# A first sweep put in another order: the loads of two chunks ahead of a weight quarter, and state steps ahead of a scan and a transpose

## The chip, the cores and the metric

The kernel runs on one core of a Trainium2 chip. Its engines each work through a stream of their own, in order, and wait for each other only through semaphores: TensorE (PE in the profile, with its weight loads as PEld), VectorE (DVE), ScalarE (ACT), GpSimd (POOL) and SyncE (SP), which issues nearly all loads and stores. The metric is the device time of one execution in microseconds, and the median of several runs is compared.

## The reference

The input goes through a Mamba-2 style recurrence with decay, and then through a two-layer network with a tanh GELU. The recurrence works on 4 batches with 8 heads, a sequence of 768, heads of 32 and a state of 16:

```python
cum = np.cumsum(la, axis=-1)                                  # la: log of the decay a, inside a chunk
M = np.einsum('bhin,bhjn->bhij', Cc, Bc) * np.exp(cum_i - cum_j) * causal
y_intra = np.einsum('bhij,bhjd->bhid', M, xc)
y_inter = np.einsum('bhin,bhnd->bhid', Cc, state) * np.exp(cum)[..., None]
y[:, :, sl] = y_intra + y_inter
state = decay_full * state + sum_j(Bc * xc * decay_from_j)
...
x = y as (3072 tokens, 256)
h = x @ w_in                                                  # 256 x 2048
g = 0.5 * h * (1 + tanh(c * (h + 0.044715 * h**3)))
return g @ w_out                                              # 2048 x 256
```

## The kernel before

The sequence of each batch is cut into 6 chunks of 128, 24 chunks in all, and two chunks make a unit, 12 units u. Each unit of 256 tokens goes through the recurrence and then through the network. Everything is cut into named steps, and a step is one Python function that issues a few instructions on one engine (lines 777 to 960 name the steps and their engines). The string `ORDERED` (line 17) is the schedule: it lists the steps in the order in which their functions are called. Since an engine takes its instructions in that order, the string fixes the order on each engine, and on SP the order of the loads. A suffix (`:A`, `:D`, `:P`) puts a step on ACT, DVE or POOL in place of its usual engine, and `~n` issues filler matmuls. The framework adds the semaphores that the data need; a DMA that takes a semaphore used by an earlier one waits for that one to land.

The steps that the change and the prediction touch:

- **Loads.** `load_wi.q` (L190) brings a quarter of w_in, 512 KB, for the columns q*512 and on. `load_bc1.i` (L154) brings B (i = 0) or C (i = 1) of chunks 4 and 5 of batch 0, 128 KB each, in pieces of 128 bytes. `load_bc0` did so for chunks 0 to 3 at the start. `load_bc.b.i`, `load_x.u` and `load_wo.q` bring B or C of a later batch, a unit's x, and a quarter of w_out.
- **Casts.** `wi.q.k` and `wo.q.k` (L343, L346) turn half a quarter of the weights into bf16, mostly on POOL; `castx.u` does so for x.
- **Decay.** `clip` and `R` (L385, L388) make the decay products of all batches by a scan along each row. `tp2` (L391) transposes those of chunks 4 and 5 in four instructions, `tp6` (L399) those of the other batches, and `recip1`, `recip.b` invert them. `pe` (L406) picks the decay at the chunk ends, `pp` (L413) spreads it over the partitions by a matmul, and `pend` (L419) copies it out of PSUM. Chunks 0 to 3 have their own, earlier `Rq`, `tpq`, `pendq`.
- **B and C of chunks 4 and 5.** `mul1.i` (L457) scales them, `T1.i` (L463) transposes them on TensorE, `bh1` and `ce1.e` (L480, L473) copy B and the two masked forms of C out of PSUM, and `N1`, `bn1` (L483, L490) make B's other form.
- **Unit steps.** `G.u` (L614) multiplies B with C, `M.u.i` (L627) masks the product, half i at a time, `S.u.k` (L692) carries the state over chunk 2u + k, `SP.c` (L704) forms the state that chunk c hands on, `D.u` (L644) adds up the chunk's own state, and `Y.u` (L657) gives the unit's output from the earlier state (L673) and the chunk itself (L682). `yev.u` copies it as bf16 into `xm`. For units 0 and 1, `XX.u`, `XD.u` and `xn.c` (L578 to L605) unpack x and do the work of `D`.
- **Network.** `s1.u.i` (L723) multiplies a unit with 256 columns of w_in, in four matmuls, and needs the w_in quarter (2i + 1) // 4, so s1.u.6 and s1.u.7 need the last one, q = 3. `gelu.u.i` (L735) takes the result from PSUM. `s2.u.k.q` (L740) multiplies with a quarter of w_out, `oev` copies out and `store` writes.

The PSUM tile `hp` has two buffers, which `s1`, `D`, `pp` and one half of `XX` share in the order of the schedule. A group that takes one waits until the step that reads the group before last is done.

Of the kernel before, what the change touches and what calls it, by code (L numbers as in the profile page):

```python
# [18 lines left out]
load_a.0 load_a.1 c_warm load_a.2:A load_a.3:A load_x4 c_sel c_cz c_bmask clipq load_wi.0 Rq tpq  # L19
recip0 c_m16 mulc.0 ~51 tw.1 ew.1.1:A mulc.1 tw.2 mulb c_sub c_unp c_ends ~4 tw.0 peq ew.0.2 ew.0.1  # L20
load_wi.1 ew.0.0:A ew.1.2 c_par ~4 G.0 x4.1 ew.1.0 x4.0:D M.0.0 ~4 ppq GE.2 GE.3 pendq XX.0 ME.2
XD.0 xn.1 ME.3 xn.0:D load_wi.2 SP.0 ~17 Y.0 wi.0.1:A wi.0.0:A S.0.0 clip R S.0.1 yev.0.0.2 wi.1.1
XX.1 XD.1 wi.1.0 tp2 wi.2.1 xn.2 s1.0.0 G.1 S.1.0 s1.0.1 xn.3 gelu.0.0 gelu.0.1 s1.0.2 gelu.0.2
M.1.1 wi.2.0 M.1.0 s1.0.3 gelu.0.3 s1.0.4 s1.0.5 recip1 S.1.1 gelu.0.4 gelu.0.5 SP.1 load_wi.3
wi.3.1 wi.3.0 load_bc1.1 s1.0.6 load_bc1.0 mul1.0:P SP.2 pe mul1.1:P T1.0 bh1:D tp6 Y.1 gelu.0.6 pp
load_wo.0 pend:D yev.1.0.2 T1.1 N1 wo.0.0 s1.0.7 load_x.2 ce1.1:D castx.2.None ce1.0:D recip.1
s1.1.0 bn1 SP.3 gelu.0.7 wo.0.1 G.2 D.2 gelu.1.0 S.2.0 s1.1.1 gelu.1.1 s2.0.0.0.o s1.1.2 gelu.1.2
s1.1.3 load_bc.1.1 SP.4 load_bc.1.0 M.2.1 M.2.0 gelu.1.3 load_wo.1 s2.0.1.0.o mul.1.0 s1.1.4
mul.1.1:P recip.2 load_x.3 gelu.1.4 wo.1.0 s1.1.5 wo.1.1 Y.2 gelu.1.5 castx.3.None s1.1.6 yev.2.0.2
T.1.0 s1.1.7 gelu.1.6 load_wo.2 E.1.0 T.1.1 s1.2.0 N.1 gelu.1.7 gelu.2.0 E.1.1 bn.1:D s1.2.1 F.1  # L30
s2.0.0.1.o wo.2.0 wo.2.1:D s1.2.2 gelu.2.1 s2.0.1.1.o D.3 G.3 S.3.0 gelu.2.2 s1.2.3 gelu.2.3 S.3.1
M.3.0 M.3.1 load_wo.3 load_x.4 wo.3.0:A s2.0.0.2.o s2.0.1.2.o wo.3.1 SP.6 s1.2.4 s1.2.5 castx.4.None
s2.0.0.3.o s2.0.1.3.o gelu.2.4 gelu.2.5 oev.0:D s1.2.6 Y.3 oev.1 yev.3.0.2:D s2.1.0.0.o s2.1.0.1.o
s2.1.0.2.o gelu.2.6 s2.1.0.3.o s1.2.7 S.4.0 oev.2 recip.3 S.4.1 s1.3.0 s2.1.1.0.o M.4.1 s2.1.1.1.o
gelu.3.0 s2.1.1.2.o gelu.2.7 s2.1.1.3.o s1.3.1 s1.3.2 gelu.3.1 gelu.3.2 oev.3:D s2.2.0.0.o
s2.2.0.1.o s1.3.3 gelu.3.3 s2.2.0.2.o load_bc.2.1 load_bc.2.0 s2.2.0.3.o mul.2.1:P s1.3.4 M.4.0
load_x.5 s1.3.5 gelu.3.4 mul.2.0:P castx.5.None:D SP.7 oev.4:D SP.8 SP.9 s2.2.1.0.o s2.2.1.1.o
gelu.3.5 s2.2.1.2.o s1.3.6 s2.2.1.3.o gelu.3.6 Y.4 load_wr.2.1 s1.3.7 oev.5:D s2.3.0.0.o yev.4.0.2
load_x.6 load_wr.2.0 S.5.0 gelu.3.7 s1.4.0 s2.3.0.1.o M.5.0 load_tr.2.1 gelu.4.0 SP.10 M.5.1 s1.4.1
s2.3.0.2.o castx.6.None s1.4.2 load_bn.2 gelu.4.1 load_tr.2.0 s1.4.3 store.0 s2.3.0.3.o gelu.4.2  # L40
# [961 lines left out]
```

## Time and profile before

| | |
|---|---|
| median of 3 runs | 117.01 us (116.45 to 117.2) |
| profiled execution | 116.76 us |
| its span (first to last instruction) | 115.0 us |
| granted TensorE clock | 1.0 |
| TensorE busy | 108.1 us, 94% of the span |
| ScalarE, VectorE, GpSimd busy | 70.0, 68.0, 25.9 us |
| HBM read and written | 11.07 MB, 3.93 MB |

The profile is of one execution. Busy times are sums over the span; an engine can be busy for most of it and still not be what the end waits for. The timeline gives start, duration and, in brackets, how long the engine stood before an instruction and what ended that time; where several semaphores were waited for, it names the one that came last by its own records. A DMA issue is shown with the time that SP took to issue it, and apart from that the time until its last byte landed.

### The profile page before, as it was taken

The page shows a single profiled execution, that of the slowest core. Times are in us where ns is not written, and L with a number is a line of the kernel's source. Part 1 is how long each engine was busy: PE and PEld are TensorE (multiplying, and loading weights), DVE is VectorE, ACT ScalarE, POOL GpSimd, SP SyncE. Part 2 cuts the span into 40 slices and gives each one's busy share as a digit, 9 for nine tenths or more (in the row PEclk, how much of TensorE's full clock was granted, in tenths as well). Part 3 has the DMA queues.
Part 4 walks back from the last instruction along what each step waited for, and adds up shares of the span by engine and source line. Part 5 has one row for each costly group of instructions (what it writes and reads, how often), then busy time and mean ns, then how long its engine had stood idle before and what let it go on. Part 6 is the DMA issues. An engine that isn't in the chain of part 4 may idle for free.

```text
span 115.0 us, 3377 instructions
## 1 busy us (share of the span) xinstructions
PE 108.1 (94%) x1421; PEld 91.7 (80%) x1421; DVE 68.0 (59%) x136; ACT 70.0 (61%) x133; POOL 25.9 (23%) x54
## 2 busy tenths in 40 slices
PE   6979888999999999999999999999999999999990
PEld 2235566888879997989989899889898898999970
DVE  6889998989974755969448491186750851010100
ACT  3159687687654455747675876456495576758620
POOL 7636856806439020201120030000000000000000
PEclk9999999999999999999999999999999999999999
DMA  0999979979994779997556922350003020001113
GB/s 24 231 309 336 332 212 191 317 132 321 215 238 101 141 177 203 196 272 175 88 131 150 209 62 85 111 86 0 0 9 134 0 71 26 0 0 55 42 62 120
DMA packets 43103, 16.00 MB, mean 139 GB/s; under 512 B 36688, under 2 KB 41552, under 8 KB 43088
## 3 DMA queue, kind: packets, MB, share of 16 engines
q1 hardware_dynamic: 42896, 15.70, 55.3%
q8 instruction: 11, 0.18, 0.7%
q10 hardware_dynamic: 192, 0.09, 0.3%
q14 instruction: 4, 0.03, 0.1%
HBM read 11.07 MB, written 3.93 MB: 130 GB/s over the span
## 4 chain that ended last, share of the span: by engine, by line
PE 82%; DVE 5%; DMA 4%; SPq 3%; issue 2%; ACT 2%; DVEq 0%
PE hp L732 35%; PE o_ps L750 34%; DMA x_t<-in_x_dram 4%; PE yb L750 3%; PE yb L673 3%; PE ga L618 2%; PE yb L682 2%; DVE m L628 1%; DVE sp_new L706 1%; SPq L164 1%; ACT gT L736 1%; SPq L151 1%; SPq L160 1%; DVE rt L364 1%; DVE r_t L354 1%
## 5 line engine op out<-in xcount | busy, mean ns | idle before, releaser
L736 ACT ACTIVATE gT<-hp 128x512 bf16<-128x512 f32 x96 | 54.3, 596 | 28.9 <-PE hp L732 28.6
L732 PE MATMUL hp<-xm,w_in_sb 128*128 128x256 bf16 x384 | 53.4, 273 | 1.1 <-DVE s_new L699 0.5
L750 PE MATMUL o_ps<-w_out_sb,gT 128*128 128x256 bf16 x352 | 46.8, 273 | 0.0
L732 PEld LDWEIGHTS <-w_in_sb 128*128 128x128 bf16 x384 | 41.2, 114 | 4.0 <-issue 2.7
L750 PEld LDWEIGHTS <-gT 128*128 128x128 bf16 x384 | 37.4, 98 | 4.1 <-issue 0.4
L341 DVE COPY o_sb<-o_ps 128x256 f32<-128x256 f32 x12 | 5.1, 425 | 26.9 <-PE o_ps L750 26.9
L628 DVE TENSOR_TENSOR m<-ga,tri 128x1024 bf16<-128x1024 f32 x12 | 14.6, 1216 | 0.0
L628 DVE TENSOR_TENSOR m<-gb,tri 128x1024 bf16<-128x1024 f32 x11 | 13.4, 1216 | 0.0
L339 POOL CAST x<-x_t 128x512 bf16<-128x512 f32 x8 | 6.0, 756 | 28.1 <-DMA x_t<-in_x_dram 24.4
L706 DVE SCALAR_TENSOR_TENSOR sp_new<-s_new,pend,bmask 128x256 bf16<-128x256 f32 x17 | 8.0, 483 | 0.1
L699 DVE SCALAR_TENSOR_TENSOR s_new<-s_new,pend,hp 128x64 f32<-128x64 f32 x13 | 3.5, 272 | 7.4 <-PE hp L651 7.3
L720 PE MATMUL yb<-wz 128*128 128x512 bf16 (+2 forms) x21 | 6.6, 455 | 1.1 <-DVE warm L226 1.1
L337 ACT ACTIVATE o_sb<-o_ps 128x256 f32<-128x256 f32 x10 | 3.8, 383 | 5.1 <-PE o_ps L750 3.8
L682 PE MATMUL yb<-m,x 128*32 128x128 bf16 x192 | 6.1, 220 | 0.0
L337 ACT ACTIVATE xm<-yb 128x512 bf16<-128x512 f32 x8 | 4.8, 596 | 1.3 <-PE hp L651 0.7
L720 PEld LDWEIGHTS <-wz 128*128 128x128 bf16 x21 | 2.3, 116 | 4.1 <-issue 2.1
L673 PE MATMUL yb<-ce,sp_new 128*32 128x128 bf16 x160 | 5.3, 221 | 0.0
L339 POOL CAST w_out_sb<-wf 128x512 bf16<-128x512 f32 x6 | 4.1, 692 | 4.7 <-DMA wf<-in_moe_w_out_dram 4.7
L618 PE MATMUL ga<-ce,bh 32*128 32x256 bf16 x48 | 4.7, 273 | 0.3 <-DVE par L289 0.3
L618 PE MATMUL gb<-ce,bh 32*128 32x256 bf16 x48 | 4.7, 273 | 0.0
L750 PE MATMUL yb<-w_out_sb,gT 128*128 128x256 bf16 x32 | 4.5, 273 | 0.0
L682 PEld LDWEIGHTS <-x 128*32 128x32 bf16 x192 | 3.7, 96 | 0.9 <-issue 0.9
(114 smaller groups left out, 75.0 us busy)
## 6 DMA issues: line engine op xcount, KB each, us to landing
out_dram<-o_sb SPq DMA_DIRECT2D x24, 128.0 KB, 2.0
x_t<-in_x_dram SPq DMA_DIRECT2D x20, 128.0 KB, 3.9
wf<-in_moe_w_in_dram SPq DMA_DIRECT2D x4, 512.0 KB, 7.0
wf<-in_moe_w_out_dram SPq DMA_DIRECT2D x4, 512.0 KB, 7.1
bc_t<-in_C_dram SPq DMA_DIRECT2D x3, 384.0 KB, 4.7
bc_t<-in_B_dram SPq DMA_DIRECT2D x3, 384.0 KB, 5.7
scr<-bc SPq DMA_DIRECT2D x4, 192.0 KB, 2.3
x_t<-in_x_dram SPq DMA_DIRECT2D x1, 512.0 KB, 4.4
```

The source lines that it names most:

```text
L337: nc.scalar.activation(o, i, AF.Copy)
L339: nc.gpsimd.tensor_copy(out=o, in_=i)
L341: nc.vector.tensor_copy(out=o, in_=i)
L618: nc.tensor.matmul(out=gbank(g)[:, 256 * k:256 * k + 256], lhsT=bh_of(2 * u + k)[gs], rhs=ce_of(2 * u + k)[gs], start=True, stop=True, til ...
L628: nc.vector.tensor_tensor(out=m_of(u)[:, 2 * i:2 * i + 2].rearrange("p g k e t -> p (g k e) t"), in0=gx[i].rearrange("p g (k t) -> p (g k) ...
L673: nc.tensor.matmul(out=y4[32 * j:32 * j + 32, k, w], lhsT=sp[:, 32 * h:32 * h + 32], rhs=ce_of(gc)[:, h % 2], start=first(j), stop=False, ...
L682: nc.tensor.matmul(out=y4[32 * j:32 * j + 32, k, w], lhsT=X16[u][:, k, 32 * h:32 * h + 32], rhs=m[:, h // 2, h % 2, :], start=first(j), st ...
L706: nc.vector.scalar_tensor_tensor(out=sp_new.rearrange("p (g d) -> p g d", g=4), in0=(XN[0][:, H * D:H * D + 64] if gc == 0 else state[("s" ...
L720: nc.tensor.matmul(out=t[:, 0:m * 128], lhsT=wz, rhs=w3.to_broadcast([128, m, 128]), start=True, stop=True, skip_group_check=True)
L732: nc.tensor.matmul(out=hp[:, j * T:(j + 1) * T], lhsT=w_in_k[:, w, q, k], rhs=xm[:, w, u * T:(u + 1) * T], start=(w == 0), stop=(w == 1))
L736: nc.scalar.activation(gts[u][:, 2 * i:2 * i + 2], hps.pop((u, i)).rearrange("p (j t) -> p j t", j=2), AF.Gelu_apprx_tanh)
L750: nc.tensor.matmul(out=ops[gc], lhsT=gts[u][:, fi, k * Q:(k + 1) * Q], rhs=w_out_sb[:, fi, :], start=(fi == 0 and (u > 0 or k == 0)), stop ...
```

## The change

Only the string `ORDERED` changes, in the part of the first w_in sweep (unit 0) and the first half of the second. `load_bc1.0` and `load_bc1.1`, in this order now, come ahead of `load_wi.3`. `S.0.1` comes ahead of `R`, `S.1.0` ahead of `tp2`, `SP.1` and `SP.2` ahead of and between `M.1.0` and `M.1.1`, which change places. `mul1.0` comes ahead of the casts of the last w_in quarter on POOL and `mul1.1` behind them. `T1.0`, `Y.1` and `pp` come ahead of `s1.0.6`, and `G.2` and `D.2` stay behind `s1.1.0`. `bh1` and `pend` go from VectorE to ScalarE, `yev.1` from ScalarE to VectorE. From `gelu.1.7` on the list is the same as before (the diff breaks its lines elsewhere).

```diff
-XD.0 xn.1 ME.3 xn.0:D load_wi.2 SP.0 ~17 Y.0 wi.0.1:A wi.0.0:A S.0.0 clip R S.0.1 yev.0.0.2 wi.1.1
-XX.1 XD.1 wi.1.0 tp2 wi.2.1 xn.2 s1.0.0 G.1 S.1.0 s1.0.1 xn.3 gelu.0.0 gelu.0.1 s1.0.2 gelu.0.2
-M.1.1 wi.2.0 M.1.0 s1.0.3 gelu.0.3 s1.0.4 s1.0.5 recip1 S.1.1 gelu.0.4 gelu.0.5 SP.1 load_wi.3
-wi.3.1 wi.3.0 load_bc1.1 s1.0.6 load_bc1.0 mul1.0:P SP.2 pe mul1.1:P T1.0 bh1:D tp6 Y.1 gelu.0.6 pp
-load_wo.0 pend:D yev.1.0.2 T1.1 N1 wo.0.0 s1.0.7 load_x.2 ce1.1:D castx.2.None ce1.0:D recip.1
-s1.1.0 bn1 SP.3 gelu.0.7 wo.0.1 G.2 D.2 gelu.1.0 S.2.0 s1.1.1 gelu.1.1 s2.0.0.0.o s1.1.2 gelu.1.2
-s1.1.3 load_bc.1.1 SP.4 load_bc.1.0 M.2.1 M.2.0 gelu.1.3 load_wo.1 s2.0.1.0.o mul.1.0 s1.1.4
-mul.1.1:P recip.2 load_x.3 gelu.1.4 wo.1.0 s1.1.5 wo.1.1 Y.2 gelu.1.5 castx.3.None s1.1.6 yev.2.0.2
-T.1.0 s1.1.7 gelu.1.6 load_wo.2 E.1.0 T.1.1 s1.2.0 N.1 gelu.1.7 gelu.2.0 E.1.1 bn.1:D s1.2.1 F.1
+XD.0 xn.1 ME.3 xn.0:D load_wi.2 SP.0 ~17 Y.0 wi.0.1:A wi.0.0:A S.0.0 clip S.0.1 R yev.0.0.2 wi.1.1
+XX.1 XD.1 xn.2 S.1.0 tp2 s1.0.0 G.1 SP.1 load_bc1.0 s1.0.1 wi.1.0 M.1.0 gelu.0.0 xn.3 s1.0.2
+gelu.0.1 gelu.0.2 s1.0.3 SP.2 M.1.1 wi.2.1 wi.2.0 mul1.0:P recip1 gelu.0.3 S.1.1 load_bc1.1
+load_wi.3 wi.3.1 s1.0.4 T1.0 load_wo.0 load_x.2 load_bc.1.1 gelu.0.4 s1.0.5 Y.1 pe gelu.0.5 pp
+wi.3.0 s1.0.6 mul1.1:P T1.1 bh1 tp6 yev.1.0.2:D ce1.1:D N1 pend gelu.0.6 bn1 ce1.0:D load_bc.1.0
+s1.0.7 wo.0.0 s1.1.0 G.2 load_wo.1 gelu.0.7 castx.2.None gelu.1.0 recip.1 SP.3 wo.0.1 D.2 S.2.0
+s1.1.1 M.2.0 s1.1.2 gelu.1.1 s2.0.0.0.o s1.1.3 SP.4 gelu.1.2 M.2.1 s2.0.1.0.o gelu.1.3 s1.1.4 s1.1.5
+mul.1.0 gelu.1.4 mul.1.1:P recip.2 wo.1.0 wo.1.1 load_x.3 Y.2 s1.1.6 T.1.0 E.1.0 castx.3.None
+gelu.1.5 yev.2.0.2 gelu.1.6 s1.1.7 T.1.1 s1.2.0 N.1 load_wo.2 gelu.1.7 gelu.2.0 E.1.1 bn.1:D s1.2.1
+F.1 s2.0.0.1.o wo.2.0 wo.2.1:D s1.2.2 gelu.2.1 s2.0.1.1.o D.3 G.3 S.3.0 gelu.2.2 s1.2.3 gelu.2.3
...
```

More of the change, by code (lines that the diff above doesn't have):

```diff
@@ L27 @@
-s1.1.0 bn1 SP.3 gelu.0.7 wo.0.1 G.2 D.2 gelu.1.0 S.2.0 s1.1.1 gelu.1.1 s2.0.0.0.o s1.1.2 gelu.1.2
-s1.1.3 load_bc.1.1 SP.4 load_bc.1.0 M.2.1 M.2.0 gelu.1.3 load_wo.1 s2.0.1.0.o mul.1.0 s1.1.4
-mul.1.1:P recip.2 load_x.3 gelu.1.4 wo.1.0 s1.1.5 wo.1.1 Y.2 gelu.1.5 castx.3.None s1.1.6 yev.2.0.2
-T.1.0 s1.1.7 gelu.1.6 load_wo.2 E.1.0 T.1.1 s1.2.0 N.1 gelu.1.7 gelu.2.0 E.1.1 bn.1:D s1.2.1 F.1
-s2.0.0.1.o wo.2.0 wo.2.1:D s1.2.2 gelu.2.1 s2.0.1.1.o D.3 G.3 S.3.0 gelu.2.2 s1.2.3 gelu.2.3 S.3.1
-M.3.0 M.3.1 load_wo.3 load_x.4 wo.3.0:A s2.0.0.2.o s2.0.1.2.o wo.3.1 SP.6 s1.2.4 s1.2.5 castx.4.None
@@ L33 @@
[L33 to L37, printed above, removed]
+XD.0 xn.1 ME.3 xn.0:D load_wi.2 SP.0 ~17 Y.0 wi.0.1:A wi.0.0:A S.0.0 clip S.0.1 R yev.0.0.2 wi.1.1
@@ new lines @@
+mul.1.0 gelu.1.4 mul.1.1:P recip.2 wo.1.0 wo.1.1 load_x.3 Y.2 s1.1.6 T.1.0 E.1.0 castx.3.None
+gelu.1.5 yev.2.0.2 gelu.1.6 s1.1.7 T.1.1 s1.2.0 N.1 load_wo.2 gelu.1.7 gelu.2.0 E.1.1 bn.1:D s1.2.1
+F.1 s2.0.0.1.o wo.2.0 wo.2.1:D s1.2.2 gelu.2.1 s2.0.1.1.o D.3 G.3 S.3.0 gelu.2.2 s1.2.3 gelu.2.3
+S.3.1 M.3.0 M.3.1 load_wo.3 load_x.4 wo.3.0:A s2.0.0.2.o s2.0.1.2.o wo.3.1 SP.6 s1.2.4 s1.2.5
+castx.4.None s2.0.0.3.o s2.0.1.3.o gelu.2.4 gelu.2.5 oev.0:D s1.2.6 Y.3 oev.1 yev.3.0.2:D s2.1.0.0.o
+s2.1.0.1.o s2.1.0.2.o gelu.2.6 s2.1.0.3.o s1.2.7 S.4.0 oev.2 recip.3 S.4.1 s1.3.0 s2.1.1.0.o M.4.1
@@ L38 @@
+s2.1.1.1.o gelu.3.0 s2.1.1.2.o gelu.2.7 s2.1.1.3.o s1.3.1 s1.3.2 gelu.3.1 gelu.3.2 oev.3:D
+s2.2.0.0.o s2.2.0.1.o s1.3.3 gelu.3.3 s2.2.0.2.o load_bc.2.1 load_bc.2.0 s2.2.0.3.o mul.2.1:P s1.3.4
+M.4.0 load_x.5 s1.3.5 gelu.3.4 mul.2.0:P castx.5.None:D SP.7 oev.4:D SP.8 SP.9 s2.2.1.0.o s2.2.1.1.o
 gelu.3.5 s2.2.1.2.o s1.3.6 s2.2.1.3.o gelu.3.6 Y.4 load_wr.2.1 s1.3.7 oev.5:D s2.3.0.0.o yev.4.0.2
```

## The prediction

> **What bounds the kernel now.** I read the page first, then windows of busy time, then the waits, then the timeline of 11 to 21 us, where the two orders differ.
>
> ```profile
> PE 108.1 (94%) x1421; PEld 91.7 (80%) x1421; DVE 68.0 (59%) x136; ACT 70.0 (61%) x133; POOL 25.9 (23%) x54
> PE 82%; DVE 5%; DMA 4%; SPq 3%; issue 2%; ACT 2%; DVEq 0%
> 12.40:17.60 5.20, 4.14 (x36) 3.11 (x36) 5.09 (x13) 4.15 (x9) 3.62 (x8) 1.00 0.95 242
> 17.60:20.70 3.10, 2.87 (x60) 2.18 (x61) 2.72 (x10) 2.38 (x5) 2.22 (x5) 1.00 1.05 215
> 24.40:112.00 87.60, 87.52 (x1126) 78.35 (x1118) 46.30 (x81) 54.08 (x102) 10.97 (x13) 1.00 0.47 110
> ```
>
> The first two rows are the page's busy times and its chain; the others are stretches, with length, then busy us and count of PE, PEld, DVE, ACT and POOL. TensorE is the bound, and from 24.40 to 112 us it is busy for 87.52 of 87.60 us. Whatever the change does is therefore carried to the end as one shift of the place where TensorE becomes dense. I take as that place the start of s1.1.1, the second group of the second w_in sweep, at 20.70 us. Before it, the first sweep has gaps, and the question is what fills them. The next fence is the timeline: start, duration, engine, line, operation, and in brackets the idle time before it with what ended it.
>
> ```profile
> 12.31 0.99 DVE L364 STREAM_TRANSPOSE rt<-r_t 32x64 f32<-32x64 f32 x4
> 12.42 0.60 PE L732 MATMUL hp<-xm,w_in_sb 128*128 128x256 bf16 x4 [0.18 <-DVE s_new L699]
> 13.33 0.28 DVE L699 SCALAR_TENSOR_TENSOR s_new<-s_new,pendq,hp 128x64 f32<-128x64 f32 x1
> 13.66 1.03 PE L732 MATMUL hp<-xm,w_in_sb 128*128 128x256 bf16 x8 [0.31 <-DVE s_new L699]
> 13.53 1.22 DVE L628 TENSOR_TENSOR m<-gb,tri 128x1024 bf16<-128x1024 f32 x1
> 14.66 1.17 POOL L339 CAST w_in_sb<-wf 128x512 bf16<-128x512 f32 x2 [0.27 <-DMA wf<-in_moe_w_in_dram]
> 14.66 1.21 DVE L628 TENSOR_TENSOR m<-ga,tri 128x1024 bf16<-128x1024 f32 x1
> 16.06 0.87 DVE L706 SCALAR_TENSOR_TENSOR sp_new<-s_new,pendq,bmask 128x256 bf16<-128x256 f32 x2
> 16.86 1.09 ACT L736 ACTIVATE gT<-hp 128x512 bf16<-128x512 f32 x2 [0.20 <-PE hp L732]
> 16.99 0.62 POOL L459 TENSOR_TENSOR bc0s<-bcf,rt 128x256 bf16<-128x256 f32 x1 [1.16 <-DVE pe L408]
> 17.04 0.64 DVE L409 TENSOR_TENSOR pe<-pe,m 128x48 f32<-128x48 f32 x1
> 17.67 0.29 PE L467 MATMUL ga<-ident,bc0s 128*128 128x128 bf16 x2 [0.36 <-DVE pe L409]
> 18.45 0.42 PE L415 MATMUL hp<-pe,selp 128*128 128x48 f32 x2
> 18.57 0.60 ACT L337 ACTIVATE xm<-yb 128x512 bf16<-128x512 f32 x1 [0.62 <-PE yb L682]
> 18.71 0.28 PE L467 MATMUL gb<-ident,bc0s 128*128 128x128 bf16 x2
> 18.93 1.04 PE L732 MATMUL hp<-xm,w_in_sb 128*128 128x256 bf16 x8
> 19.07 0.87 DVE L478 TENSOR_SCALAR ce<-gb,par 128x256 bf16<-128x256 bf16 x2
> 19.13 0.38 ACT L337 ACTIVATE bn<-ga 128x256 bf16<-128x256 bf16 x1
> 19.57 1.08 ACT L736 ACTIVATE gT<-hp 128x512 bf16<-128x512 f32 x2
> 20.00 0.28 PE L618 MATMUL ga<-ce,bh 32*128 32x256 bf16 x2
> 20.70 0.60 PE L732 MATMUL hp<-xm,w_in_sb 128*128 128x256 bf16 x4
> ```
>
> Two stops are what the change is aimed at. S.1.0 (DVE, 13.33) stands behind tp2 (the four transposes at 12.31), and s1.0.1 (PE, 13.66) waits for the PSUM buffer that S.1.0 frees. And T1.0 (PE, 17.67) waits for mul1.0 (POOL, 16.99). The page puts that wait down to pe, but mul1.0 does not read pe: it reads rt, written by tp2 at 13.30, and the B of chunks 4 and 5. So I go to the DMA issues, with start and time taken, and then the time from issue to landing of each.
>
> ```profile
> 6.52 0.56 SPq L192 DMA_DIRECT2D wf<-in_moe_w_in_dram  x1
> wf<-in_moe_w_in_dram SPq DMA_DIRECT2D x1, 512.0 KB, 8.1
> 7.12 0.47 SPq L156 DMA_DIRECT2D bcf<-in_C_dram  x1
> bcf<-in_C_dram SPq DMA_DIRECT2D x1, 128.0 KB, 9.5
> 7.63 3.38 SPq L156 DMA_DIRECT2D bcf<-in_B_dram  x1
> bcf<-in_B_dram SPq DMA_DIRECT2D x1, 128.0 KB, 9.2
> q8 instruction: 1, 0.02, 6.0%
> ```
>
> The last w_in quarter (wi.3) lands at 6.52 + 8.1 = 14.6, C at 16.6 and B at 7.63 + 9.2 = 16.8, just ahead of mul1.0. They land in the order of issue. The last row is the DMA view of 14.5 to 15.5 us: one instruction fetch used 6.0% of 16 engines for 1 us, which is one engine for 0.96 us.
>
> **The change part by part.** Nothing is added or removed; the same instructions are issued in another order, and three go to another engine.
>
> *State steps.* S.0.1 goes ahead of R, S.1.0 ahead of tp2, SP.1 and SP.2 ahead of and between the two M of unit 1. S.1.0 can then run when XD.1 is done, about 12.3. s1.0.0 starts some 0.15 earlier (its 0.18 wait), and s1.0.1 at about 13.25 in place of 13.66: 0.4 gained there. tp2 pays the 0.2 of S.1.0, which mul1.0 does not feel. DVE's own sum up to pe does not shrink, since it had no gap (5.09 of 5.20 us busy). Start to start the rows give 0.20 for S.1.0 (13.33 to 13.53), 1.02 for tp2, 1.13 for one M (13.53 to 14.66), 1.40 for the other with recip1 and S.1.1 (14.66 to 16.06), and 1.62 for both SP and pe (16.06 to 17.04 + 0.64 = 17.68). From 12.31 on that is 17.68 in any order, which is where pe ended before.
>
> *Loads.* B (now first), then C, then wi.3. The likely landings are B near 14.0 and C near 14.5, with wi.3 last. For wi.3 the low bound is 14.6 plus 256 KB at the 404 GB/s of the row below, 15.3. The high bound is 16.85 plus another 0.75, if the fetch of 0.96 falls on its engine and the order costs more: 17.6. I take 16.9, because the same three loads and the same fetch pass through the same engines, and the last of them ended at 16.85.
>
> ```profile
> 12.00:13.00 1.00, 0.82 (x41) 0.54 (x44) 0.94 (x5) 0.69 (x3) 1.00 (x2) 1.00 1.05 404
> ```
>
> The Trainium skill, "DMA: Bandwidth & Descriptors", section "Specifications", says that transfers need pieces of 512 B or more for full rate. By that the pair would hold wi.3 back by more than the 0.65 us of its bytes; here 256 KB took 16.85 - 14.61 = 2.24 us, so the trace agrees, though the fetch is in it.
>
> *TensorE up to pp.* mul1.0 follows the four earlier w_in casts on POOL at 14.4 and ends at 15.0. PE then goes s1.0.2 (13.7), s1.0.3 (14.5) and s1.0.4 (15.0), each held by the gelu that frees its buffer, T1.0 (15.5, 2.2 earlier), s1.0.5 (15.7), Y.1 when the second M is done (16.8 to 17.2). Then it stands at pp until pe is done: 17.68 + 0.04 = 17.72. So the gains come to a stop at an instruction of DVE that comes no earlier than before.
>
> *What was early and becomes late.* s1.0.6 reads wi.3, and ran at 16.7 before. Now it is behind pp: 17.72 + 0.26 = 17.98 (pp to T1.1, 18.45 to 18.71). And it waits for wi.3's two casts: 16.9 + 0.05 + 1.17 + 0.05 = 18.17, say 18.2 (0.05 from landing 14.61 to cast 14.66). The pair of casts has taken the place of mul1.0 after the last landing, and mul1.1 stands behind both on POOL: 18.12 + 0.62 = 18.74, so T1.1 goes at 18.8 against 18.71. Behind T1.1 wait N1, s1.0.7 and s1.1.0 on PE, and ce1 on DVE, then G.2: 0.1 later, 20.1.
>
> *Engines changed.* bh1 and pend go from DVE to ACT, and yev.1 from ACT to DVE. On DVE, tp6 and yev.1 (0.52, and 0.69 for a like cast at 33.40, rows below) follow pe and end near 18.9, before ce1 can start at 19.1: no cost, with 0.2 of cover. On ACT pend comes after pp (out at 17.72 + 0.42 = 18.14). Its two copies were not seen on ACT: they lie between 0.17 each, as pendq's small one, and 0.38, as bn1. I take 0.2, the nearer in size, so ACT is free at 18.6 for gelu.0.6 at 18.8; at 0.38 it would be 0.1 later.
>
> ```profile
> 18.34 0.52 DVE L364 STREAM_TRANSPOSE rt<-r_t 128x192 f32<-128x192 f32 x1
> 33.40 0.69 DVE L341 CAST xm<-yb 128x512 bf16<-128x512 f32 x1 [0.55 <-PE hp L651]
> 9.95 0.17 ACT L337 ACTIVATE pendq<-hp 128x4 f32<-128x4 f32 x1
> ```
>
> *Sum.* s1.0.6 starts at 18.2, its last product is out 0.60 later, and ACT goes gelu.0.6 (18.82), bn1 (+0.56, as yev.1 to bn1 before, 18.57 to 19.13), gelu.0.7 (+0.44, as 19.13 to 19.57) = 19.82. Before, gelu.0.7 began at 19.57. s1.1.1 needs gelu.1.0's buffer and began 1.13 after gelu.0.7; so it starts at 20.95, **0.25 later than 20.70**. The road over G.2 gives 0.1. If wi.3 lands at 15.3, pp alone sets s1.0.6, 0.2 earlier, and the shift is near 0; at 17.6 it is 0.25 + 0.7 = 0.95. Everything behind keeps its order. The later loads (wo.0, x.2, bc.1) carry the same bytes in the same order and don't come later; M.2 and Y.2 shift along.
>
> The profiled execution took 116.76 (span 115.0, 1.76 around it), which gives 117.01. It lies 0.25 under the median of 117.01, so I carry the shift to that: 117.26, and forecast **117.2**.
>
> **The rivals.**
>
> *A. The gaps do close (faster).* For it: T1.0 and Y.1 move 2.2 and 1 us forward, and TensorE has 5.20 - 4.14 = 1.06 us idle in 12.40 to 17.60. It decides if pe ends by 17.2 and wi.3 lands by 16.2. Then s1.0.6 would start right behind Y.1 and pp, at 17.5, 0.7 earlier than I have it: 117.26 - 0.7 = 116.5. Against it: DVE is busy 5.09 of 5.20 us there, and pe is at the end of that.
>
> *B. wi.3 is the new wait (slower).* One engine's share of it lands late, by the fetch or by an issue that is held up, as B's was for 3.38 us. From 16.9 on, each us of delay is one us of s1.0.6. At 18.0 the time is 117.26 + 1.1 = 118.4.
>
> *C. The load order does nothing.* If B still lands at 16.8, T1.0 stays at 17.67, and behind it come Y.1 (0.78 up to pp, 17.67 to 18.45), s1.0.5 (0.44, half of the eight matmuls in the row below) and pp (0.26). s1.0.6 goes at 19.15, 0.95 later than forecast: 118.2.
>
> ```profile
> 21.73 0.87 PE hp L732 x8
> ```
>
> Against C: in the trace, loads land in order of issue.
>
> *D. The clock falls (slower).* TensorE's work up to 20.70 is spread otherwise, and the granted clock, 1.00 in every row above, could drop in a thin stretch. At half clock the sixteen matmuls of four groups of 0.44 cost another 1.8 us: 119. Its point would be a stretch with far less work than 4.14 of 5.20 us; I find no gap over 0.7 us. The Trainium skill, "TensorE: Matmul & The Clock Gate", "Part 1: The HAM clock gate", puts the drop after an idle window of some 3.4 us; no stretch here is idle for that, and the trace so far agrees.
>
> **How the numbers follow.** Forecast 0.70, A 0.11, B 0.10, C 0.05, D 0.04. A measurement of this kernel tells some 1% (1.17 us) from no change; its three runs spread over 0.75. The range goes from A's 116.5 less 0.2 of spread, 116.3, to B's 118.4, and leaves out D and the far ends of A and B. Over 1% faster (under 115.84) needs twice the idle time that A can take: 0.05. Over 1% slower (118.18) is D, most of B and some of C: 0.15. Within 1%: 0.80.
>
> **What would show it.** Right: T1.0 near 15.5, an idle TensorE ahead of pp (L415) ended by pe (L409) near 17.7, POOL's last two w_in casts near 17, s1.0.6 at 18.2, s1.1.1 at 20.9 to 21.0, and 87.6 us from there on unchanged. Wrong: wi.3's casts before 16 or after 17.7, pp before 17.4, s1.1.1 before 20.5, or a new gap behind 24.4.

## The result, and the profile after

The changed kernel took 118.53 us in the median of 6 runs (117.74 to 119.56), against 117.11 us (116.45 to 117.76, 6 runs) for the kernel before on the same chip. The ratio is 1.0109, with a 95% interval of 1.0065 to 1.0153. Here and below, a ratio leaves out executions that took over 1.5% more than their kernel's shortest, and a median does not, so the ratio is not the quotient of the medians. The change makes the kernel slower by about 1.3 us, where 0.25 had been forecast.

The profiled execution took 119.56 us (span 117.8). The page of it, busy times and one load:

```profile
PE 109.2 (93%) x1421; PEld 92.2 (78%) x1421; DVE 68.6 (58%) x134; ACT 69.8 (59%) x135; POOL 25.3 (21%) x54
x_t<-in_x_dram SPq DMA_DIRECT2D x1, 512.0 KB, 6.7
```

TensorE is the bound as before. The last row shows something else: in this execution the first load of x took 6.7 us to land, against 4.4 in the profile before, and everything behind it lies about 2 us later. That is no effect of the change, since in a second profiled execution of the same kernel (first experiment, 118.25 us) it took 4.4 us again. So for places in time I use that second execution too. A stretch behind the first sweep (length, busy us and count of PE, PEld, DVE, ACT and POOL, clock, DMA share, GB/s), and then the timeline of this profile (start, duration, engine, line, operation, idle time before it and what ended that):

```profile
27.00:114.00 87.00, 87.00 (x1133) 77.95 (x1121) 47.26 (x81) 54.19 (x101) 10.17 (x13) 1.00 0.47 109
```

```profile
11.37 3.17 SPq L192 DMA_DIRECT2D wf<-in_moe_w_in_dram  x1
15.07 0.28 DVE L699 SCALAR_TENSOR_TENSOR s_new<-s_new,pendq,hp 128x64 f32<-128x64 f32 x1 [0.42 <-ACT x L337]
18.07 0.27 PE L467 MATMUL ga<-ident,bc0s 128*128 128x128 bf16 x2 [0.31 <-DVE m L628]
18.47 1.17 POOL L339 CAST w_in_sb<-wf 128x512 bf16<-128x512 f32 x2 [1.10 <-DMA wf<-in_moe_w_in_dram]
20.62 0.39 PE L415 MATMUL hp<-pe,selp 128*128 128x48 f32 x2 [0.56 <-DVE pe L409]
23.41 1.03 PE L732 MATMUL hp<-xm,w_in_sb 128*128 128x256 bf16 x8 [0.21 <-ACT gT L736]
```

From 27 to 114 us TensorE is busy for the whole time, so the loss is again a shift of the start of s1.1.1 (last row). Two rows speak of the change's two parts. The issue of wi.3, at 11.37, took SP 3.17 us; before, it came at 6.52 and took 0.56. The issue of a load is the time for which SP is occupied with it; the load lands later. And S.1.0 (15.07), with tp2 behind it now, stands for xn.2, a copy on ScalarE from which it needs no data. POOL waits 1.10 us for wi.3 (18.47), and TensorE 0.56 us for pe (20.62).

### The profile page after: what moved, and what is told of

Read it like the earlier page. It is cut to its first block, busy times and chain, and to the rows that moved or that the text cites. A ratio compares the mean times of both kernels' runs of the same rounds, so it can differ in the third digit from the quotient of the medians.

```text
span 117.8 us, 3377 instructions
## 1 busy us (share of the span) xinstructions
PE 109.2 (93%) x1421; PEld 92.2 (78%) x1421; DVE 68.6 (58%) x134; ACT 69.8 (59%) x135; POOL 25.3 (21%) x54
## 4 chain that ended last, share of the span: by engine, by line
PE 81%; DMA 6%; DVE 4%; ACT 3%; SPq 2%; issue 1%
PE hp L732 34%; PE o_ps L750 33%; DMA x_t<-in_x_dram 6%; PE yb L750 3%; PE yb L682 3%; PE ga L618 2%; PE yb L673 2%; DVE m L628 2%; ACT gT L736 1%; PE yb L720 1%; SPq L164 1%; SPq L151 1%; DVE rt L364 1%; DVE sp_new L706 1%; SPq L160 1%
## 5 line engine op out<-in xcount | busy, mean ns | idle before, releaser
L339 POOL CAST x<-x_t 128x512 bf16<-128x512 f32 x8 | 5.5, 687 | 28.6 <-DMA x_t<-in_x_dram 21.5
L720 PE MATMUL yb<-wz 128*128 128x512 bf16 (+2 forms) x21 | 7.9, 524 | 1.1 <-DVE warm L226 1.1
L706 DVE SCALAR_TENSOR_TENSOR sp_new<-s_new,pend,bmask 128x256 bf16<-128x256 f32 x17 | 8.6, 519 | 0.1
L337 ACT ACTIVATE xm<-yb 128x512 bf16<-128x512 f32 x7 | 4.2, 596 | 0.7 <-PE hp L651 0.7
```

What stands on the lines that cost most here:

```text
L337: nc.scalar.activation(o, i, AF.Copy)
L339: nc.gpsimd.tensor_copy(out=o, in_=i)
L706: nc.vector.scalar_tensor_tensor(out=sp_new.rearrange("p (g d) -> p g d", g=4), in0=(XN[0][:, H * D:H * D + 64] if gc == 0 else state[("s" ...
L720: nc.tensor.matmul(out=t[:, 0:m * 128], lhsT=wz, rhs=w3.to_broadcast([128, m, 128]), start=True, stop=True, skip_group_check=True)
```

## The experiments

Theories: **H**, wi.3 is late because its issue is held up behind two small loads; **R**, S.1.0 and with it tp2 and pe are late because S.1.0 must wait until xn.2 has read the same PSUM buffer. Rivals: the loss is chance of one execution; the loss is wi.3's bytes alone, in the size forecast; the three steps that changed engines cost it. Each ratio is against the kernel before on the same chip.

**The changed kernel again**, without an edit.

> The changed kernel once more, for a second trace. In the first one, one engine's share of x4 landed at 10.67 us where it was 8.43 before, and all that follows was 2.2 us late; wi.3 was issued from 11.37 to 14.54 and landed at 18.41. Theory H (the issue of wi.3 is held up behind the two loads in small pieces): without a late x4, wi.3's issue still takes over 2.5 us, and wi.3 lands 3 us or more behind C, at 17.2 to 17.8; s1.1.1 starts at 21.5 to 22.0; time 1.0% over before. Rival F (as forecast: the same bytes through the same engines): wi.3 lands at 16.9, within 1.5 us behind C, s1.1.1 at 20.95; then the measured 1% is the late x4 alone, and the time is 0.2 to 0.4% over before.

118.07 us, ratio 1.0121 (1.0085 to 1.0157): the loss is not the chance of one execution. SP's issues with start and time taken, and the time to landing, in this execution:

```profile
6.20 0.37 SPq L156 DMA_DIRECT2D bcf<-in_B_dram  x1
6.62 3.99 SPq L156 DMA_DIRECT2D bcf<-in_C_dram  x1
10.65 3.15 SPq L192 DMA_DIRECT2D wf<-in_moe_w_in_dram  x1
wf<-in_moe_w_in_dram SPq DMA_DIRECT2D x1, 512.0 KB, 7.2
```

SP is stopped in the issue of C and again in that of wi.3, which so lands at 10.65 + 7.2 = 17.9. Its casts, pe and pp follow here at:

```profile
11.34 1.15 ACT L337 ACTIVATE w_in_sb<-wf 128x512 bf16<-128x512 f32 x2 [0.87 <-DMA wf<-in_moe_w_in_dram]
13.28 0.28 DVE L699 SCALAR_TENSOR_TENSOR s_new<-s_new,pendq,hp 128x64 f32<-128x64 f32 x1 [1.28 <-ACT x L337]
17.94 1.17 POOL L339 CAST w_in_sb<-wf 128x512 bf16<-128x512 f32 x2 [1.95 <-DMA wf<-in_moe_w_in_dram]
19.31 0.39 PE L415 MATMUL hp<-pe,selp 128*128 128x48 f32 x2 [0.62 <-DVE pe L409]
22.11 1.03 PE L732 MATMUL hp<-xm,w_in_sb 128*128 128x256 bf16 x8
```

wi.3's casts (to 19.11) and pp (19.31, with s1.0.6 behind it at 19.54) both come late, by about the same: both theories have a place in this trace, and the next runs part them. s1.1.1 starts at 22.11, 1.41 later than before, and the span is 1.5 longer. About 0.55 of the 1.28 us before S.1.0 are this execution's own: ScalarE stood 0.87 us for the first w_in quarter (11.34), and xn.2 is behind its casts. With that quarter in time the same order made S.1.0 stand 0.73 us in two other experiments.

Did the engines idle while SP was stopped? Stretches of 1 us, last the busy share of the 16 DMA engines and GB/s, of the kernel before (the share adds up transfers that overlap, so it can pass 1):

```profile
13.00:14.00 1.00, 0.69 (x13) 0.52 (x13) 0.95 (x4) 0.66 (x2) 0.85 (x3) 1.00 1.23 275
14.00:15.00 1.00, 0.75 (x8) 0.59 (x6) 1.00 (x2) 0.70 (x2) 0.73 (x2) 1.00 1.02 153
```

and of this execution of the changed one:

```profile
13.00:14.00 1.00, 0.97 (x13) 0.57 (x13) 0.67 (x3) 0.59 (x2) 0.90 (x2) 1.00 0.44 79
14.00:15.00 1.00, 0.95 (x8) 0.79 (x8) 0.94 (x4) 0.98 (x3) 0.94 (x2) 1.00 0.46 108
```

The share falls from 1.23 and 1.02 to 0.44 and 0.46. So the DMA engines were not full in these 2 us; that they had too little to move because SP had not issued it is what H says.

**The load order alone, in the kernel before.**

```diff
-... recip1 S.1.1 gelu.0.4 gelu.0.5 SP.1 load_wi.3
-wi.3.1 wi.3.0 load_bc1.1 s1.0.6 load_bc1.0 mul1.0:P
+... recip1 S.1.1 gelu.0.4 gelu.0.5 SP.1 load_bc1.0
+load_bc1.1 load_wi.3 wi.3.1 wi.3.0 s1.0.6 mul1.0:P
```

> The kernel before with only the loads moved: B and C of chunks 4 and 5 ahead of wi.3 on SP, every other engine in the order of before. mul1 stands behind the two casts of wi.3 on POOL here. Theory H: wi.3 lands at 17.2 to 17.8, s1.0.6 and T1.0 behind it, T1.0 at 19.3 to 19.8 in place of 17.67; 1.3 to 2% slower than before. Rival F: wi.3 at 16.9, s1.0.6 at 18.2, T1.0 at 18.8, about 1.0 us (0.9%) slower. If the loads cost nothing, 0%.

120.13 us, 1.0261 (1.0154 to 1.0369). wi.3 was issued from 9.96 to 13.67 and landed at 17.7. In this order mul1.0 stands behind wi.3's casts, so T1.0 came at 19.52, and more hangs on the landing than in the changed kernel. And something else appeared, in stretches of 3.41 us:

```profile
16.31:19.72 3.41, 1.18 (x10) 0.62 (x8) 0.79 (x4) 0.96 (x3) 2.01 (x4) 1.00 0.98 261
19.72:23.13 3.41, 3.41 (x48) 2.72 (x46) 2.58 (x8) 1.90 (x4) 2.23 (x5) 0.50 1.12 257
```

While TensorE waited for wi.3 it was busy for 1.18 of 3.41 us, and after that its clock was granted at 0.50 for 3.41 us. So the 2.6%, more than either theory had, are not the price of the order alone. Nor is the clock all of it: one of the four executions took 120.12 us at a mean clock of 1.0.

**The state steps alone, in the kernel before.**

```diff
-XD.0 ... clip R S.0.1 yev.0.0.2 wi.1.1
-XX.1 XD.1 wi.1.0 tp2 wi.2.1 xn.2 s1.0.0 G.1 S.1.0 s1.0.1
+XD.0 ... clip S.0.1 R yev.0.0.2 wi.1.1
+XX.1 XD.1 wi.1.0 xn.2 S.1.0 tp2 wi.2.1 s1.0.0 G.1 s1.0.1
```

> The kernel before with only three steps moved: S.0.1 ahead of R, xn.2 and S.1.0 ahead of tp2. s1.0.1 should start near 13.25 in place of 13.66, tp2 0.2 later. Theories H and F both: T1.0 still waits for B at 16.8, so the 0.4 us are lost in that wait and the time is that of before, -0.1 to +0.1%. If the gap at 13.3 was worth its length, 0.35% faster.

118.03 us, 1.0082 (1.0027 to 1.0137). With the loads as before, this part alone makes the kernel slower, which neither theory had forecast. Its timeline:

```profile
12.91 0.28 DVE L699 SCALAR_TENSOR_TENSOR s_new<-s_new,pendq,hp 128x64 f32<-128x64 f32 x1 [0.73 <-ACT x L337]
13.23 0.99 DVE L364 STREAM_TRANSPOSE rt<-r_t 32x64 f32<-32x64 f32 x4
13.25 1.04 PE L732 MATMUL hp<-xm,w_in_sb 128*128 128x256 bf16 x8
17.71 0.80 POOL L459 TENSOR_TENSOR bc0s<-bcf,pt 128x256 bf16<-128x256 f32 x1
17.95 0.57 DVE L408 TENSOR_TENSOR pe<-ac,r_t 128x3 f32<-128x3 f32 x1
18.45 0.60 POOL L339 CAST w_out_sb<-wf 128x512 bf16<-128x512 f32 x1
18.56 0.56 DVE L409 TENSOR_TENSOR pe<-pe,m 128x48 f32<-128x48 f32 x1
19.27 0.39 PE L415 MATMUL hp<-pe,selp 128*128 128x48 f32 x2 [0.62 <-DVE pe L409]
```

s1.0.1 starts at 13.25, as forecast. But VectorE stood 0.73 us before S.1.0, and tp2 starts at 13.23 in place of 12.31. The first operation of pe, on 3 numbers per partition, took 0.57 us here; I come back to that. pp starts at 19.27, 0.82 later than before, and s1.1.1 at 21.49, 0.79 later.

**S.1.0 listed ahead of xn.2, in the changed kernel**, so that it need not wait for that copy.

```diff
-XX.1 XD.1 xn.2 S.1.0 tp2 s1.0.0
+XX.1 XD.1 S.1.0 xn.2 tp2 s1.0.0
```

> The changed kernel with one step moved by one place: S.1.0 ahead of xn.2 in the list, so that VectorE's S.1.0 waits for TensorE alone and ScalarE's xn.2, which reads the same PSUM buffer, waits for S.1.0. In the traces of the changed kernel and of the state steps alone, VectorE stood 0.73 to 1.28 us before S.1.0, until xn.2 was done. Theory R (S.1.0 waits for the other reader of its buffer): that stop falls to 0.2 us or less, pe and pp come 0.6 earlier against R (scan), but wi.3 still lands near 17.7, so s1.0.6 gains at most 0.2: 0 to 0.3% faster than the changed kernel. Rival P (VectorE waits for TensorE's XD.1 there): the stop stays at 0.7.

118.24 us, 1.011 (1.0031 to 1.0189).

```profile
12.46 0.28 DVE L699 SCALAR_TENSOR_TENSOR s_new<-s_new,pendq,hp 128x64 f32<-128x64 f32 x1 [0.32 <-PE hp L596]
12.77 0.38 ACT L337 ACTIVATE x<-hp 128x256 bf16<-128x256 f32 x1 [0.62 <-DVE s_new L699]
```

The wait has turned round: now the copy waits for S.1.0, and S.1.0 for the matmul only. Two engines that read the same PSUM tile are kept in the order of the list, though neither writes it; that is what R said. It does not pay. S.1.0 still stands 0.32 us for TensorE, and tp2 starts at 12.77. wi.3, issued from 8.99 to 13.34, lands at 17.2, and pe lies beside its casts on GpSimd (17.22 to 18.39): its two operations took 0.49 and 0.56 us, and pp comes at 18.59. Behind that, D.2 waits for x of unit 2, and s1.1.1 starts at 21.78:

```profile
21.63 0.21 PE L651 MATMUL hp<-x,bn 128*32 128x64 bf16 x4 [0.60 <-POOL x L339]
```

**A square of four.** The loads in the order B, wi.3, C; the state steps put back; and both. The fourth corner is the changed kernel.

```diff
-... S.1.1 load_bc1.1
-load_wi.3 wi.3.1 s1.0.4
+... S.1.1 load_wi.3
+load_bc1.1 wi.3.1 s1.0.4
```

> The changed kernel with one load put back: B, then wi.3, then C, so that one load in small pieces stands ahead of wi.3 and not two. T1.0 needs B, T1.1 needs C. Theory H: wi.3 is issued without a long hold, lands near 15.5, and pp becomes the bound: s1.0.6 near 18.0, C at 16.9 is early enough for mul1.1; 0.7 to 1.2% faster than the changed kernel, and within 0.3% of before. Rival F: all three landed by 16.9 as in the changed kernel, with wi.3 ahead: s1.0.6 0.2 us earlier, 0.2% faster than the changed kernel.

```diff
-... clip S.0.1 R yev.0.0.2 wi.1.1
-XX.1 XD.1 xn.2 S.1.0 tp2 s1.0.0 G.1 SP.1 load_bc1.0
+... clip R S.0.1 yev.0.0.2 wi.1.1
+XX.1 XD.1 xn.2 tp2 s1.0.0 G.1 S.1.0 SP.1 load_bc1.0
```

> The changed kernel with S.0.1 behind R and S.1.0 behind tp2 again, the loads left as changed. Theories H and R: VectorE has no stop before tp2 and pe ends near 17.7 to 18.0; wi.3 lands near 17.7 and alone sets s1.0.6, at 19.0 to 19.2; 0.3 to 0.5% faster than the changed kernel, 0.7 to 0.9% slower than before. If the state steps were the whole loss, the time is that of before.

> Both undone in part: S.0.1 and S.1.0 back behind R and tp2, and the loads as B, wi.3, C. Theories H and R: wi.3 lands near 16.0, pe ends near 17.7, pp decides, s1.0.6 near 18.0, s1.1.1 at 20.6 to 20.9; the time of before within 0.3%, 1% faster than the changed kernel. If something else in the changed order costs time (the three steps on other engines, POOL beside VectorE), it stays 0.5% or more over before.

| ratio (95% interval) | state steps as changed | state steps back |
|---|---|---|
| B, C, wi.3 | 1.0121 (1.0085 to 1.0157) | 1.0053 (1.0006 to 1.0101) |
| B, wi.3, C | 1.0070 (1.0046 to 1.0094) | 1.0003 (0.9974 to 1.0031) |

C ahead of wi.3 costs 0.5% in both columns, the state steps 0.7% in both rows, and without the two the rest of the change, engines included, costs nothing that the interval can tell. Each single difference is near what its intervals can tell, and the 0.5% of the right column is within them; but the pairs agree. The columns come from two chips, each set beside the kernel before there, and the corner of 1.0070 rests on two executions. The traces agree in kind: with B, wi.3, C, the state steps as changed put pp at 18.49 and s1.1.1 at 21.28, against 18.05 and 20.85 with them back, which is 0.43 us or 0.4%. There wi.3 landed at 16.0 and 15.6.

With the state steps back and C ahead of wi.3 the trace shows how the loads act by themselves:

```profile
6.83 2.07 SPq L156 DMA_DIRECT2D bcf<-in_C_dram  x1
8.95 4.40 SPq L192 DMA_DIRECT2D wf<-in_moe_w_in_dram  x1
17.22 1.17 POOL L339 CAST w_in_sb<-wf 128x512 bf16<-128x512 f32 x2 [1.64 <-DMA wf<-in_moe_w_in_dram]
18.44 0.63 PE L732 MATMUL hp<-xm,w_in_sb 128*128 128x256 bf16 x4
20.50 0.86 POOL L339 CAST x<-x_t 128x512 bf16<-128x512 f32 x1 [0.98 <-DMA x_t<-in_x_dram]
21.41 0.21 PE L651 MATMUL hp<-x,bn 128*32 128x64 bf16 x4 [0.73 <-POOL x L339]
21.56 1.06 PE L732 MATMUL hp<-xm,w_in_sb 128*128 128x256 bf16 x8
```

With B, wi.3, C in the same kernel:

```profile
6.74 3.47 SPq L192 DMA_DIRECT2D wf<-in_moe_w_in_dram  x1
17.22 0.62 POOL L459 TENSOR_TENSOR bc0s<-bcf,pt 128x256 bf16<-128x256 f32 x1 [0.35 <-DVE pt L397]
17.36 0.55 DVE L409 TENSOR_TENSOR pe<-pe,m 128x48 f32<-128x48 f32 x1
18.05 0.39 PE L415 MATMUL hp<-pe,selp 128*128 128x48 f32 x2 [0.56 <-DVE pe L409]
18.28 0.60 PE L732 MATMUL hp<-xm,w_in_sb 128*128 128x256 bf16 x4
20.85 1.03 PE L732 MATMUL hp<-xm,w_in_sb 128*128 128x256 bf16 x8 [0.21 <-ACT gT L736]
```

s1.1.1 goes from 20.85 to 21.56, and only 0.16 of that comes over s1.0.6 (18.28 to 18.44). The larger part comes from x of unit 2: its load follows wi.3 and wo.0 on SP, its cast starts at 20.50 (19.19 with B, wi.3, C), and D.2 waits 0.73 us for it (21.41). That load was itself issued by 15.60, against 15.77 there. But from 13 to 16 us the share of the DMA engines was 0.48, 0.81 and 0.81, against 1.15, 1.06 and 1.08, so by my estimate 1.2 us of their time were missing, about what x landed later. So a stop at SP can make a load late that is issued well after it.

**The engines put back in the changed kernel.**

```diff
-s1.0.6 mul1.1:P T1.1 bh1 tp6 yev.1.0.2:D ce1.1:D N1 pend gelu.0.6
+s1.0.6 mul1.1:P T1.1 bh1:D tp6 yev.1.0.2 ce1.1:D N1 pend:D gelu.0.6
```

> The changed kernel with bh1 and pend on VectorE and yev.1 on ScalarE again, everything else as changed. Theory (the loads' order and the wait of S.1.0 for xn.2 make the whole loss, the engines none): as slow as the changed kernel, 1.008 to 1.016 of before, with s1.0.6 still behind pp and the late w_in quarter. Rival (the move of the three steps costs by itself, through ScalarE's pend and bh1 ahead of gelu.0.6): 0.3% or more of the loss goes, 1.008 or less, and gelu.0.6 starts sooner behind s1.0.6 than in the changed kernel.

119.59 us, 1.017 (1.0026 to 1.0314): no gain, though the interval is wide. Three of the four executions show a mean clock of 0.986; the one at 1.0 took 118.35 us, 1.0% more than the mean of the four of the kernel before at 1.0 on that chip (117.19), as the theory had it. The execution shows wi.3 in its pure form, with pp in time:

```profile
17.67 0.21 DVE L409 TENSOR_TENSOR pe<-pe,m 128x48 f32<-128x48 f32 x1
18.02 0.39 PE L415 MATMUL hp<-pe,selp 128*128 128x48 f32 x2 [0.21 <-DVE pe L409]
18.64 1.16 POOL L339 CAST w_in_sb<-wf 128x512 bf16<-128x512 f32 x2 [2.94 <-DMA wf<-in_moe_w_in_dram]
19.86 0.67 PE L732 MATMUL hp<-xm,w_in_sb 128*128 128x256 bf16 x4 [1.45 <-POOL w_in_sb L339]
```

TensorE waits 1.45 us for the casts; then its clock fell here too (below).

**An attempt to use both lessons.** From the corner of 1.0003, pe goes ahead of SP.2 and recip1 ahead of M.1.1, Y.1 behind s1.0.6, and pend, tp6 and gelu.0.6 are shifted to suit.

```diff
-gelu.0.1 gelu.0.2 s1.0.3 SP.2 M.1.1 wi.2.1 wi.2.0 mul1.0:P recip1 gelu.0.3
+gelu.0.1 gelu.0.2 s1.0.3 pe SP.2 recip1 M.1.1 wi.2.1 wi.2.0 mul1.0:P gelu.0.3
...
-s1.0.5 Y.1 pe gelu.0.5 pp wi.3.0 s1.0.6 mul1.1:P
+s1.0.5 gelu.0.5 pp wi.3.0 s1.0.6 Y.1 mul1.1:P
```

> The kernel of e9 with what is then last taken out of the way: pe between the two M of unit 1, pp and s1.0.6 ahead of Y.1, recip1 ahead of the second M, tp6 behind ce1. If wi.3 near 16.0 and pe near 15.9 are the only bounds, s1.0.6 starts at 17.3 to 17.5, T1.1 at 18.0 to 18.3, s1.1.1 at 20.0 to 20.2: 0.4 to 0.6% faster than before. If VectorE's sum still decides, the time of before.

117.3 us, 1.0035 (0.9997 to 1.0073): no better. pp came at 17.00, but in the profiled execution wi.3's casts began at 17.78 only, and TensorE stood 1.58 us before s1.0.6, with Y.1 not there to fill the time. That execution took 118.78 us, so it does not stand for the median. It shows a limit of H: the issue of wi.3 had ended at 9.31 (6.89 + 2.42), and it landed at 17.7 (6.89 + 10.8) all the same. What held it there is not shown.

**pe ahead of recip1, in the corner of 1.0003**, to test what made pe long.

```diff
-... wi.2.0 mul1.0:P recip1 gelu.0.3 S.1.1
+... wi.2.0 mul1.0:P pe recip1 gelu.0.3 S.1.1
```

> The kernel of the run with the state steps back and the loads as B, w_in quarter, C, and in it pe ahead of recip1, so that pe comes 0.26 us earlier on VectorE and mul1.1, which needs recip1, can only start behind it. Theory (an operation of VectorE with two SBUF inputs stands while GpSimd works: pe's second operation ended 0.05 to 0.07 us after GpSimd's operation in the runs so far): with GpSimd idle beside it pe takes 0.15 + 0.21 us as where GpSimd was idle, pp starts near 17.4 to 17.5 in place of 18.05, s1.0.6 near 17.7, and up to 0.5 us are gained, ratio to before 0.996 to 0.999. Rival (the 0.55 us are pe's own time): pp near 17.8, and a ratio of 0.999 to 1.001.

116.81 us, 0.9992 (0.9965 to 1.0019).

```profile
17.02 0.15 DVE L408 TENSOR_TENSOR pe<-ac,r_t 128x3 f32<-128x3 f32 x1
17.21 0.21 DVE L409 TENSOR_TENSOR pe<-pe,m 128x48 f32<-128x48 f32 x1
17.56 0.41 PE L415 MATMUL hp<-pe,selp 128*128 128x48 f32 x2
20.37 1.03 PE L732 MATMUL hp<-xm,w_in_sb 128*128 128x256 bf16 x8 [0.21 <-ACT gT L736]
24.95 0.51 PE L508 MATMUL ga<-ident,bc 128*128 128x128 bf16 x6 [0.23 <-DVE bc L499]
```

With GpSimd idle beside it pe takes 0.15 + 0.21 us, pp starts 0.49 earlier than in that corner, and s1.1.1 0.48 earlier, 0.33 earlier than in the kernel before. Most of it is given back: TensorE then waits 0.23 us at T.1.0 of batch 1 (24.95), and the time is that of before within its interval.

## Why the prediction was right or wrong

*The bound* held: TensorE, dense behind the first sweep, and one shift carried to the end.

*State steps.* s1.0.1 at 13.25 came true where the part was tried alone. "S.1.0 can then run when XD.1 is done, about 12.3" failed: it ran at 12.91 there and 13.28 in the changed kernel (0.55 of that for the late w_in quarter), because xn.2 reads the same PSUM buffer and is listed ahead of it. Free of that it still ran at 12.46. In the kernel before, tp2 filled this time. So "tp2 pays the 0.2 of S.1.0" was 0.92 in the kernel with this part alone (12.31 to 13.23). "DVE's sum up to pe does not shrink, since it had no gap" was right of before and wrong of after: the move itself opened the gap.

*pe ends 17.68 in any order* failed for a second reason. The 0.64 us of pe in the quoted row were no price of an operation: it ended at 17.68, 0.07 behind mul1.0 on GpSimd (16.99 + 0.62). Its own time is 0.21. Which operations of VectorE lie beside GpSimd depends on the order: SP.2 took 0.87 us beside mul1.0 in the corner of 1.0003, in place of about 0.47. pp was forecast for 17.72 and came at 18.04 to 18.05 with the state steps back, and with them at 18.49 to 19.31 where GpSimd worked beside pe (18.02 where it was idle), the execution with the late x left out.

*Loads.* B near 14.0 and C near 14.5 were right with the state steps back (6.42 + 7.6 and 6.83 + 7.8); in the two profiles of the changed kernel B landed at 14.4 and 15.1 and C at 16.2 and 15.8, with no harm seen. wi.3 was forecast at 16.9, with a high bound of 17.6, "because the same three loads and the same fetch pass through the same engines". Behind B and C it landed at 17.2 to 17.9 in four executions and at 18.4 and 18.6 in two, and its casts began after 17.7 in both profiles of the changed kernel (17.94 and 18.47), which the prediction had named as a sign of being wrong. The step that failed is that one: the hold-up of 3.38 us was in the quoted rows, but I moved B and left its hold-up behind as a thing of B's. It belongs to what comes next on SP. Before, that was the rest of B and then wo.0, which nobody awaited. Rival B had the clause, "by an issue that is held up", at 0.10.

*What becomes late.* s1.0.6 behind wi.3's casts was right as a mechanism: 18.44 against 18.2 with the state steps back. In the changed kernel the casts ended at 19.1, and pp, which began at 19.3, was the last.

*Engines changed* cost nothing, as forecast: the corner with them stands at 1.0003.

*The later loads "don't come later"* failed: in the trace with the state steps back, x of unit 2 made 0.55 of the 0.71 us. In the two profiles of the changed kernel D.2 did not wait for it.

*Sum.* Of the +0.25 the sign was right. The size was not: in the square the changed kernel lost 1.2% or 1.4 us, 0.5% from the loads and 0.7% from the state steps; the one part was mis-sized, the other put at nothing, since pe was to end at 17.68 in any order. The forecast time of 117.2 is to be set beside 117.01 x 1.0109 = 118.3, just inside the range; it lies on the edge of the case "slower by over 1%", which had 0.15. That it lies inside is partly luck: the top of the range was rival B's wait for wi.3 alone, and over half of the loss, by the ratios, came from the state steps.

*Rivals.* A did not come: pe was the end, and later than thought. C did not: T1.0 went at 15.7 to 16.7 (18.07 in the execution with the late x), so the B load did what it was to do. D shows in neither profile of the changed kernel, but in two of the experiments. By their mean clocks it also came in one of ten executions of the changed kernel (120.06 us at 0.986) and in seven of the kernel before (0.957 to 0.986), so it is not the change's alone.

## What to carry to other kernels

A load moved ahead of another moves its hold-up at the issuing engine too: look for the long issue in the queue, ask which load will stand there instead, and who waits for that one and for all behind it. Before an instruction is moved up, list who else touches its buffer, readers included, and see what filled the time it now stands in. And before a duration is added to a sum, see whether the instruction ended on its own or just behind another engine's.

## What the runs showed of the hardware

**SP is stopped behind loads in small pieces.** With B and C, in pieces of 128 bytes, issued one after the other, the second and the load behind it took 2.07 to 3.99 and 3.15 to 4.40 us to issue, against 0.37 to 0.56 for a free one. SP's waits for semaphores between 5.5 and 15 us, 0.4 us at most, do not explain that. When the issue of wi.3 ended after 13 us, it landed 3.8 to 4.1 us later in five executions and 5.1 in one. With B alone ahead of it, its issue took 2.08 to 3.47 us, and it landed at 15.0 to 16.0 in three executions and at 17.7 in one. Which limit is full when SP stands, no trace here shows.

**VectorE stands for GpSimd.** pe's second operation took 0.21 us with GpSimd idle and 0.52 to 0.64 beside a cast or a multiplication there, ending 0.05 to 0.07 us behind it; the first took 0.15 or 0.16, and 0.21, 0.49 and 0.57 in three runs in which GpSimd was at work when it began. The Trainium skill, "SBUF — State Buffer", "Who interferes with whom", says that an operation of VectorE with two inputs in SBUF contends with one of GpSimd that reads SBUF, and it calls the pair of ports that they share an exclusive lock. The traces agree, and the run with pe ahead of recip1 was forecast from it (pp at 17.4 to 17.5; 17.56 measured).

**The clock.** With the engines put back, stretches of 3.41 us:

```profile
16.90:20.31 3.41, 1.30 (x26) 0.95 (x25) 1.70 (x7) 0.86 (x2) 1.67 (x3) 1.00 0.83 209
20.31:23.72 3.41, 3.24 (x26) 1.69 (x24) 1.75 (x6) 2.09 (x4) 2.39 (x5) 0.50 1.07 266
```

and in the first profile of the changed kernel, where TensorE stood behind the late load of x:

```profile
8.00:11.41 3.41, 0.88 (x13) 0.65 (x15) 1.20 (x4) 1.12 (x4) 0.70 (x8) 1.00 1.00 338
```

With the load order alone and with the engines put back, 3.41 us with 1.18 and 1.30 us of TensorE's work were followed by half clock for 3.41 us, which takes some 1.7 us of work from a full TensorE. The Trainium skill, "TensorE: Matmul & The Clock Gate", "Part 1: The HAM clock gate", gives a window of about 3.4 us, and the traces agree; but it speaks of an idle window, and here a third of it busy did not keep the clock, after a gap of 1.45 us. The prediction left D aside partly on that rule. Yet the last row has less work still, 0.88 us, and the clock stayed at 1.00 behind it. So the work in any one stretch of that length does not decide alone, and no limit can be read from these runs.
